# A fused attention and GEGLU kernel: block 4 in six Strassen pairs, with the loads and the attention of batches 5 to 7 moved

## The chip, the cores and the metric

The kernel runs on one core of one Trainium2 chip. The time is the device time of one execution in microseconds, and a kernel's time is the median of several executions. Times before: 305.1, 305.68 and 306.09 us, median 305.68 us.

## What is computed

First a linear attention over 8 batches, 8 heads, 576 tokens and 64 columns a head, then a gated feed-forward layer on all 4608 tokens (512 columns in, 1536 hidden, 512 out). Cut to what matters:

```python
theta = np.pi / 2 * np.arange(S) / S
phi = lambda x: concat([relu(x) * cos(theta), relu(x) * sin(theta)])   # 64 -> 128 features
kv  = einsum('bhsf,bhsd->bhfd', phi(k), v);  z = phi(k).sum(over s)
attn = (phi(q) @ kv) / (phi(q) @ z + 1e-6)
x = attn as (B * S, H * D)
out = (gelu(x @ w_gate) * (x @ w_val)) @ w_out
```

Inputs and output are float32; the matmuls take bf16.

## The kernel before

The feed-forward layer works on nine blocks of 512 tokens (n = 0 to 8). A block has 12 hidden tiles of 128 columns (jt = 0 to 11). The attention works on batches of 576 tokens, so it runs beside the feed-forward layer of earlier tokens: while block n is computed, batch n + 1 is finished and batch n + 2 is loaded and scaled. The whole order is written out by hand: the scheduler keeps each engine's instructions in the order of the code. A place in it is a slot (n, jt).

**Gate and value, two ways.** A plain unit (`gv_unit`, L425) makes one hidden tile by 8 matmuls of 512 columns (L435), one GELU (L444, ACT) and one product (L447, DVE). A pair (`Pair`, L648) makes two hidden tiles together by a Strassen scheme with 7 products of 4 matmuls of 256 columns (L659). Products 3, 5, 6 and 7 read sums of weights (S1 to S4, `w_sum`, L618), and products 4 to 7 read differences of x parts (T1 to T4, `x_sum`, L627, on POOL). Around the products ACT copies two partial sums (L678, L682) and makes two GELUs (L691, L695), and DVE makes two sums (L686, L699) and two products (L700, L704). `step` (L709) orders one pair: product 1; product 7 of the pair before it ("old", which writes its value sum to bank 6); product 5; the first slot; product 6; the old pair's product 4; product 2; numerators, where the table has one for the second slot's number; the second slot; product 3. Numerators of an even slot run only when there is no old pair. With `std` set, the step finishes its own pair, and a plain unit and a third slot follow (up to L735); the next step then has no old pair.

Blocks 3 and 4 (n < `FULL`, 5) have five pairs and two plain units (tiles 10 and 11); blocks 5 to 8 have six pairs. The sums of the weights of tiles 10 and 11 (columns from `WX` = 1280 on) lie in the stage of v, `st[:, 2]`, in its first 1024 of 2304 float32 columns (`w_part`, L603). They are made on POOL in slots (5, 7) to (5, 10), after v of batch 7, the last, has been cast out of that stage.

**A slot** (`slot`, L1133) runs `o_step` (the output layer of the block before: one Strassen product of 6 matmuls, L552, or two; h sums on POOL, L534; stores), then `attention` (L1111), then `more` (x sums and weight sums on POOL). `attention` may turn q (`TURN`: two DMA transposes on SP's queue, L224, into the one qT buffer), transpose finished rows x into the next block's xT (`turn_x`, L383, SP's queue), start loads (`LOADS`, L98, SP's queue), run the k-v unit (`KV`, L266: 72 matmuls, L272, into banks 6 and 7, two ACT copies, L281), scale q and k (`PREPS`, `LAST`: `prep_both`, L193, on ACT) and cast v (`cast_v`, L210, on POOL, into the one vx buffer).

**Numerators** (`nm_unit`, L311): for 128 tokens of a batch, 8 matmuls against qT (L313) into banks 6 and 7, then three DVE operations (L327 to L329) that write a row tile x. `NM` tells in which slot; (5, 0) there means batch 5, tokens 0 to 127.

SP's queue is one list in order: loads, stores, transposes. A DMA on it waits, among other things, for the one eight places before it to land.

Of the kernel before, what the change touches and what calls it, by code (L numbers as in the profile page):

```python
# [16 lines left out]
def kernel(  # L17
# [55 lines left out]
    def rows(t, b):  # L73
        return t[b].rearrange("(m i) (p j) d -> (i p) m (j d)", i=2, j=R)
# [5 lines left out]
    st = inp.tile([128, 3, NP, R * D], FP32)  # L80
# [25 lines left out]
    WJ, WX = 1024, 1280  # L106
# [46 lines left out]
    vx = consts.tile([128, NP, R, D + 1], BF16)  # L153
# [31 lines left out]
    def prep_both(b, part, j, eng):  # L185
        for name in "qk":
            phi_tile(name, b)
        o = phis[:, b % 2:b % 2 + 2, :, j, part * D:(part + 1) * D]
        o = o.rearrange("p a m d -> p (a m) d")
        i = st[:, 0:2, :, j * D:(j + 1) * D].rearrange("p a m d -> p (a m) d")  # L190
        tab = (cos_t, sin_t)[part]
        if eng is nc.scalar:
            nc.scalar.activation(o, i, AF.Relu, scale=tab[:, j:j + 1])  # L193
        else:
            eng.tensor_scalar(o, i, 0.0, tab[:, j:j + 1], op0=ALU.max, op1=ALU.mult)
# [13 lines left out]
    def cast_v(b, m0, m1, copy, j0=0, j1=R):  # L209
        copy(  # L210
            vx[:, m0:m1, j0:j1, 0:D],
            staged["v", b][:, m0:m1, j0 * D:j1 * D].rearrange("p m (j d) -> p m j d", d=D),
        )
# [8 lines left out]
    def turn_q(b):  # L222
        for i in range(2):
            nc.sync.dma_start_transpose(  # L224
                out=qt_tile(b)[:, i].rearrange("f m (j p) -> f (m j) p", p=64),
                in_=phi["q", b][64 * i:64 * i + 64].rearrange("p m j f -> p (m j f)"),
            )
# [38 lines left out]
    def kv_unit(b):  # L266
        kp = phi["k", b]
        for m in range(NP):
            for j in range(R):
                for i in range(2):  # L270
                    rr = slice(64 * i, 64 * i + 64)
                    nc.tensor.matmul(  # L272
                        bank(6 + i)[:, m * (D + 1):(m + 1) * (D + 1)],
                        lhsT=kp[rr, m, j, :],
                        rhs=vx[rr, m, j, :],
                        start=(j == 0),
                        stop=(j == R - 1),
                    )
# [181 lines left out]
    def flush(engs=(nc.sync, nc.sync)):  # L460
        for i, o_sb in stores:
            store(engs, i, o_sb)
        stores.clear()
# [154 lines left out]
    def w_sum(name, j0, j1, eng=nc.vector):  # L618
        x, y, op = {
            "S1": ("A21", "A22", ALU.add),  # L620
            "S2": ("S1", "A11", ALU.subtract),
            "S3": ("A11", "A21", ALU.subtract),
            "S4": ("A12", "S2", ALU.subtract),
        }[name]
        eng.tensor_tensor(w_part(name, j0, j1), w_part(x, j0, j1), w_part(y, j0, j1), op=op)
# [266 lines left out]
    def js(a, b):  # L892
# [7 lines left out]
        (2, 10): [(5, "q", 0, 5), (5, "k", 0, 5)],  # L900
        (3, 1): [(5, "q", 5, R), (5, "k", 5, R), (5, "v")],
        (3, 9): [(6, "q", 0, 5), (6, "k", 0, 5)],
        (4, 0): [(6, "q", 5, R), (6, "k", 5, R), (6, "v")],
        (4, 9): [(7, "q", 0, 5), (7, "k", 0, 5)], (4, 10): [(7, "v")],
        (5, 0): [(7, "q", 5, R), (7, "k", 5, R)],
    }
    SUMS = {
        2: {0: "1", 1: "2", 2: "34", 3: "567"},
# [6 lines left out]
    MORE = {}  # L915
# [1 line left out]
        for i in range(4):  # L917
            MORE.setdefault((n - 1, 8 + i * (n > 3)), []).append((n, i))
    for i, name in enumerate(("S1", "S2", "S4", "S3")):
        MORE.setdefault((5, 7 + i), []).insert(0, (name, WX, J))  # L920
    for i in range(4):
        MORE.setdefault((6, min(10 + i, 11)), []).append((7, i))
        MORE.setdefault((7, 8 + i), []).append((8, i))
# [12 lines left out]
    def o_step(n, jt):  # L936
# [6 lines left out]
        if jt % 3 == 1:  # L943
            flush()

    def start_loads(n, jt):
        for b, name, *part in LOADS.get((n, jt), ()):
            if len(part) == 1:
                load(nc.sync, name, b, part[0], part[0] + 2)
            elif part:  # L950
                load(nc.sync, name, b, 0, NP, *part)
            else:
                for m in (0, 2):
                    load(nc.sync, name, b, m, m + 2)
# [18 lines left out]
    def block1():  # L973
        b, n = 2, 1
        for jt in range(JT):
# [33 lines left out]
            if jt == 11:  # L1009
                nm_unit(b, 3, 6)  # L1010
            start_loads(n, jt)

    EARLY = {
# [4 lines left out]
    def early(jt):  # L1018
        for what in EARLY.get(jt, "").split():
            part = "cs".index(what[0])  # L1020
            prep_both(4, part, int(what[1]), nc.scalar if part or jt != 7 else nc.gpsimd)

    def block2():
# [54 lines left out]
        9: "s5 c5", 10: "s6", "m11": "c6", 11: "s7 c7 s8 c8",  # L1078
    }
    LAST = {  # L1080
        2: "s0 c0", 3: "s1", 4: "c1 s2", 5: "c2", 6: "s3 c3", 7: "s4", 8: "c4 s5", 9: "c5",
        10: "s6 c6", 11: "s7", 12: "c7 s8", 13: "c8",
    }
    turns = []

    def preps(n, jt):
        if n == 2:
            early(jt)
        if n in (3, 4):
            for what in PREPS.get(jt, "").split():  # L1090
                prep_both(n + 2, "cs".index(what[0]), int(what[1]), nc.scalar)
        if n in (5, 6):
            for what in LAST.get(jt + JT * (n - 5), "").split():
                prep_both(7, "cs".index(what[0]), int(what[1]), nc.scalar)

    FULL = 5
    NM = {(3, 0): (3, 4), (4, 0): (4, 4), (5, 0): (5, 4), (5, 7): (6, 0), (5, 9): (6, 1), (5, 11): (6, 2)}
    for n in (3, 4):
        NM.update({(n, 6): (n + 1, 0), (n, 8): (n + 1, 1), (n, 10): (n + 1, 2), (n, 11): (n + 1, 3)})
    LATE = {(6, 1): (6, 3), (6, 3): (6, 4)}  # L1100
    LATE.update({divmod(6 * JT + 9 + 2 * i, JT): (7, i) for i in range(NT)})

    def numerators(n, jt, at=NM):
        if (n, jt) in at:
            nm_unit(*at[n, jt])
            turns.append(at[n, jt])

    TURN = {(3, 1): 4, (4, 0): 5, (5, 0): 6, (6, 3): 7}
    KV = {(3, 1): 4, (4, 1): 5, (5, 1): 6, (6, 5): 7}

    def attention(n, jt):  # L1111
        made = list(turns)
        numerators(n, jt, LATE)
        if (n, jt) == (3, 0):
            early(JT)
        if n == 3 and 2 < jt < 7:
            w_sum(("S1", "S2", "S4", "S3")[jt - 3], WJ, WX, eng=nc.gpsimd)
        if (n, jt) in TURN:
            turn_q(TURN[n, jt])
            start_loads(n, jt)  # L1120
        for bt in made:
            turn_x(*bt)
            turns.remove(bt)
        if (n, jt) not in TURN:
            start_loads(n, jt)
        if (n, jt) in KV:
            kv_unit(KV[n, jt])
        preps(n, jt)
        m = 2 * (jt - (7 if n < 5 else 3))
        if 3 <= n <= 5 and m in (0, 2):  # L1130
            cast_v(n + 2, m, m + 2, nc.gpsimd.tensor_copy)

    def slot(n, jt):  # L1133
        o_step(*divmod(n * JT + jt - 1, JT))
        attention(n, jt)
        more(n, jt)
        if n == NB - 1 and jt in (9, 10):
            h_sum(n, jt - 9, "S3", eng=nc.gpsimd)
        if n == NB - 1 and jt == 11:
            for name in ("S1", "S2", "S4"):  # L1140
                h_sum(n, 0, name, 0, JH - 2, eng=nc.gpsimd)
# [9 lines left out]
    for n in range(3, NB):  # L1151
        jt = 0
        for T in range(JT // 2):
            std = {2: 10, 4: 11}.get(T) if n < FULL else None
            if n < FULL and T == 5:
                break
# [4 lines left out]
            jt = jts.stop  # L1161
# [17 lines left out]
    for what in (  # L1179
# [3 lines left out]
        if isinstance(what, str):  # L1183
            p = "ST".index(what[0])
# [33 lines left out]
```

## Time and profile before

| what | us |
|---|---|
| median of three runs | 305.68 |
| the profiled execution | 304.65 |
| its span, first to last instruction | 302.9 |
| PE matmuls busy | 293.1 |
| DVE busy | 229.4 |
| ACT busy | 204.8 |
| POOL busy | 174.3 |

The profile is of one execution. PE is TensorE with its matmuls, PEld its weight loads, DVE VectorE, ACT ScalarE, POOL GpSimd, SP the engine that issues most DMAs. Times within the span count from its start. A row of the timeline or of the chain of waits gives start, length, engine, line, operation, tiles written and read, and a count of merged instructions; in the chain a piece begins where the piece before it ended. The granted clock is 0.999 over the span. Block 4's first product starts at 140.7 us, block 5's at 171.4.

### The profile page before, as it was taken

How to read it: one execution, taken by the hardware profiler on the slowest of the kernel's cores; microseconds unless marked ns; L12 is line 12 of the kernel's file. 1: busy time of each engine (PE TensorE's matmuls, PEld its weight loads, DVE VectorE, ACT ScalarE, POOL GpSimd, SP SyncE). 2: the span in 40 equal slices, each digit the busy share in tenths (PEclk: the TensorE clock that was granted, in tenths of full speed). 3: DMA queues.
4: the chain of work that ended last, by engine and by line, in shares of the span. 5: the costliest groups of instructions: out<-in, count | busy, mean ns of one | idle time of the engine just before them, and what ended most of it. 6: DMA issues, size and time to landing. Idle time of an engine off the chain costs nothing.

```text
span 302.9 us, 8135 instructions
## 1 busy us (share of the span) xinstructions
PE 293.1 (97%) x3129; PEld 232.2 (77%) x3145; DVE 229.4 (76%) x500; ACT 204.8 (68%) x405; POOL 174.3 (58%) x146
## 2 busy tenths in 40 slices
PE   7799999999999999999999999999999999999993
PEld 3584456745788778797878788988888988888882
DVE  5866995998985775879587967897669785666782
ACT  7865592997574897878687868886455546555630
POOL 5585450000029999957943797769516965496310
PEclk9999999999999999999999999999999999999999
DMA  7999999989899999997897899423943241303035
GB/s 260 265 172 208 345 294 385 306 193 226 177 179 257 216 307 183 228 272 224 118 257 237 253 253 220 113 52 78 145 85 73 52 76 25 70 3 69 2 85 124
DMA packets 73175, 53.68 MB, mean 177 GB/s; under 512 B 45392, under 2 KB 62544, under 8 KB 73136
## 3 DMA queue, kind: packets, MB, share of 16 engines
q1 hardware_dynamic: 63360, 41.17, 58.9%
q0 software_dynamic: 9696, 11.93, 17.2%
q8 instruction: 24, 0.39, 0.5%
q14 instruction: 15, 0.12, 0.1%
q10 hardware_dynamic: 80, 0.07, 0.1%
HBM read 37.75 MB, written 9.44 MB: 156 GB/s over the span
## 4 chain that ended last, share of the span: by engine, by line
PE 82%; issue 5%; DVE 5%; DMA 3%; ACT 2%; POOL 1%; SPq 1%; POOLq 0%; DVEq 0%; ACTq 0%
PE ps L659 36%; PE ps L552 21%; PE ps L435 14%; PE ps L468 3%; PE ps L313 3%; DMA st<-in_v_dram 3%; PE ps L272 3%; DVE hT L447 1%; POOL st L534 1%; PE ps L235 1%; PE ps L406 1%; ACT phis L179 1%; DVE phis L181 1%; ACT gel L444 1%; PE ps L391 1%
## 5 line engine op out<-in xcount | busy, mean ns | idle before, releaser
L639 POOL TENSOR_TENSOR fs<-xT 128x512 bf16<-128x512 bf16 x14 | 16.1, 1153 | 61.1 <-ACT vx L210 43.5
L534 POOL TENSOR_TENSOR sm<-hT 128x768 bf16<-128x768 bf16 x26 | 42.7, 1643 | 14.0 <-PE ps L659 7.8
L659 PE MATMUL ps<-fs,ws 128*128 128x256 bf16 x312 | 44.5, 273 | 0.0
L659 PEld LDWEIGHTS <-ws 128*128 128x128 bf16 x416 | 39.4, 98 | 5.6 <-issue 0.5
L659 PE MATMUL ps<-xT,wg_sb 128*128 128x256 bf16 x288 | 43.2, 272 | 0.0
L699 DVE TENSOR_TENSOR ps<-fs,ps 128x512 f32<-128x512 f32 x36 | 25.0, 695 | 23.3 <-PE ps L659 22.0
L435 PE MATMUL ps<-xT,wv_sb 128*128 128x512 bf16 (+1 forms) x159 | 35.9, 347 | 0.1
L435 PE MATMUL ps<-xT,wg_sb 128*128 128x512 bf16 (+1 forms) x149 | 34.9, 345 | 0.6
L552 PEld LDWEIGHTS <-sm 128*128 128x128 bf16 x336 | 32.4, 98 | 3.9
L691 ACT ACTIVATE gel<-ps 128x512 f32<-128x512 f32 x36 | 21.4, 594 | 18.4 <-PE ps L659 18.3
L682 ACT COPY fs<-ps 128x512 f32<-128x512 f32 x36 | 21.1, 587 | 18.1 <-DVE ps L699 17.2
L659 PEld LDWEIGHTS <-wg_sb 128*128 128x128 bf16 x288 | 28.1, 98 | 4.9 <-issue 0.3
L565 DVE TENSOR_TENSOR o_sb<-sm,ps 128x256 f32<-128x256 f32 x56 | 23.4, 418 | 10.3 <-ACT sm L570 9.5
L447 DVE TENSOR_TENSOR hT<-gel,ps 128x512 bf16<-128x512 f32 (+1 forms) x40 | 23.9, 604 | 9.2 <-PE ps L435 6.8
L552 PEld LDWEIGHTS <-hT 128*128 128x128 bf16 x288 | 27.9, 98 | 3.8 <-issue 0.2
L444 ACT ACTIVATE gel<-ps 128x512 f32<-128x512 f32 (+1 forms) x40 | 21.1, 535 | 11.9 <-PE ps L435 11.0
L700 DVE TENSOR_TENSOR hT<-gel,ps 128x512 bf16<-128x512 f32 x36 | 24.7, 687 | 3.5
L534 POOL TENSOR_TENSOR sm<-hT,sm 128x768 bf16<-128x768 bf16 x12 | 19.7, 1644 | 12.9 <-PE ps L552 12.9
L695 ACT ACTIVATE gel<-ps 128x512 f32<-128x512 f32 x36 | 21.5, 598 | 7.9 <-PE ps L659 6.3
L686 DVE TENSOR_TENSOR ps<-fs,ps 128x512 f32<-128x512 f32 x36 | 24.9, 691 | 1.5 <-PE ps L659 0.8
L329 DVE TENSOR_TENSOR x_sb<-ps,rec 128x512 bf16<-128x512 f32 x36 | 24.9, 691 | 1.4 <-DVE rec L328 0.2
L193 ACT ACTIVATE phis<-st,sin_t 128x512 bf16<-128x512 f32 x36 | 25.6, 721 | 0.0
(137 smaller groups left out, 633.1 us busy)
## 6 DMA issues: line engine op xcount, KB each, us to landing
out_dram<-o_sb SPq DMA_DIRECT2D x69, 128.0 KB, 2.5
st<-in_v_dram SPq DMA_DIRECT2D x10, 576.0 KB, 6.3
st<-in_q_dram SPq DMA_DIRECT2D x5, 640.0 KB, 4.9
st<-in_q_dram SPq DMA_DIRECT2D x5, 512.0 KB, 5.2
st<-in_k_dram SPq DMA_DIRECT2D x4, 640.0 KB, 6.0
st<-in_k_dram SPq DMA_DIRECT2D x4, 576.0 KB, 4.7
st<-in_q_dram POOLq DMA_DIRECT2D x4, 576.0 KB, 12.1
st<-in_k_dram SPq DMA_DIRECT2D x4, 512.0 KB, 5.5
```

What stands on the lines that cost most here:

```text
L193: nc.scalar.activation(o, i, AF.Relu, scale=tab[:, j:j + 1])
L329: nc.vector.tensor_tensor(x, nm[:, :, :, 0:D], rec[:, :, :, None].to_broadcast([128, 2, 4, D]), op=ALU.mult,)
L435: nc.tensor.matmul(bank(to[g])[:, 0:w], lhsT=wt[:, ct, js], rhs=xt[:, ct, c0:c0 + w], start=(ct == 0), stop=(ct == CT - 1),)
L444: nc.scalar.activation(gel[:, 0:w], bank(to[0])[:, 0:w], AF.Gelu)
L447: nc.vector.tensor_mul(hT[n][:, jt, c0:c0 + w], gel[:, 0:w], bank(to[1])[:, 0:w])
L534: eng.tensor_tensor(a[name][:, j0:j1], a[x][:, j0:j1], a[y][:, j0:j1], op=op)
L552: nc.tensor.matmul(at, lhsT=hs.setdefault(key, h_parts(n, p))[a][:, j], rhs=ts[b][:, j], start=(j == 0 and i in ((1, 2, 4, 5), (1, 4, 5))[ ...
L565: nc.vector.tensor_tensor(o, got[key, k], x, op=op)
L659: nc.tensor.matmul(to[:, 256 * half:256 * half + 256], lhsT=w_part(a, j * 128, (j + 1) * 128)[:, ct], rhs=xb[self.n][b][:, ct], start=(hal ...
L686: nc.vector.tensor_tensor(bank(MIX), self.m5, self.sum, op=ALU.add)
L699: nc.vector.tensor_tensor(bank(val), self.m5, self.sum, op=ALU.add)
L700: nc.vector.tensor_tensor(self.h(1), both(gel1), both(bank(val)), op=ALU.mult)
```

## The change

Block 4 gets six pairs in place of five pairs and two plain units. For that the weight sums of tiles 10 and 11 are made in slots (4, 7) to (4, 10), so the stage of v must be free by then: v of batch 6 is loaded in slot (3, 10) in place of (4, 0) and cast in (4, 3) and (4, 4) in place of (4, 7) and (4, 8). The stage is not free again for a whole v: batch 7's is loaded in halves (two head pairs each) into columns 1024 to 2175, in (4, 10) and (5, 4), and cast in (5, 3) and (5, 7), in place of one load in (4, 10) with casts in (5, 3) and (5, 4).

Block 4's numerators move from even to odd slots: batch 5's from (4, 6), (4, 8), (4, 10), (4, 11) to (4, 5), (4, 7), (4, 9), (4, 11), and its last from (5, 0) to (5, 1). The turn of q of batch 6 moves from (5, 0) to (5, 1), and so do the later parts of q and k of batch 7. The scaling of batch 6 is spread from (4, 2) to (5, 0) and that of batch 7 from (5, 4) to (6, 2), before (5, 2) to (6, 1). Blocks 0 to 3 keep their products; blocks 6 to 8 keep their order apart from the scaling's end.

```diff
-        (4, 0): [(6, "q", 5, R), (6, "k", 5, R), (6, "v")],
-        (4, 9): [(7, "q", 0, 5), (7, "k", 0, 5)], (4, 10): [(7, "v")],
-        (5, 0): [(7, "q", 5, R), (7, "k", 5, R)],
+        (3, 10): [(6, "v")], (4, 0): [(6, "q", 5, R), (6, "k", 5, R)],
+        (4, 9): [(7, "q", 0, 5), (7, "k", 0, 5)], (4, 10): [(7, "half", 0)],
+        (5, 1): [(7, "q", 5, R), (7, "k", 5, R)], (5, 4): [(7, "half", 2)],
...
-        MORE.setdefault((5, 7 + i), []).insert(0, (name, WX, J))
+        MORE.setdefault((4, 7 + i), []).insert(0, (name, WX, J))
...
+    half = st[:, 2].rearrange("p m x -> p (m x)")[:, 1024:1024 + 2 * R * D]
+    half = half.rearrange("p (m x) -> p m x", m=2)
+    def cast_half(b, m):
+        nc.gpsimd.tensor_copy(
+            vx[:, m:m + 2, :, 0:D], half.rearrange("p m (j d) -> p m j d", d=D)
+        )
...
+            if name == "half":
+                nc.sync.dma_start(out=half, in_=rows(v, b)[:, part[0]:part[0] + 2])
+            elif len(part) == 1:
...
     LAST = {
-        2: "s0 c0", 3: "s1", 4: "c1 s2", 5: "c2", 6: "s3 c3", 7: "s4", 8: "c4 s5", 9: "c5",
-        10: "s6 c6", 11: "s7", 12: "c7 s8", 13: "c8",
+        6: {
+            2: "s0 c0", 3: "s1", 4: "c1 s2", 5: "c2", 6: "s3 c3", 7: "s4", 8: "c4 s5",
+            9: "c5 s6", 10: "c6 s7", 11: "c7", 12: "s8 c8",
+        },
+        7: {
+            16: "s0 c0", 17: "s1", 18: "c1 s2", 19: "c2", 20: "s3 c3", 21: "s4", 22: "c4 s5",
+            23: "c5 s6", 24: "c6 s7", 25: "c7", 26: "s8 c8",
+        },
...
-        if n in (3, 4):
+        if n == 3:
...
+        for b in LAST:
+            for what in LAST[b].get(jt + JT * (n - 4), "").split() if isinstance(jt, int) else ():
+                prep_both(b, "cs".index(what[0]), int(what[1]), nc.scalar)
...
-    FULL = 5
-    NM = {(3, 0): (3, 4), (4, 0): (4, 4), (5, 0): (5, 4), (5, 7): (6, 0), (5, 9): (6, 1), (5, 11): (6, 2)}
-    for n in (3, 4):
-        NM.update({(n, 6): (n + 1, 0), (n, 8): (n + 1, 1), (n, 10): (n + 1, 2), (n, 11): (n + 1, 3)})
+    FULL = 4
+    NM = {
+        (3, 0): (3, 4), (3, 6): (4, 0), (3, 8): (4, 1), (3, 10): (4, 2), (3, 11): (4, 3),
+        (4, 0): (4, 4), (4, 5): (5, 0), (4, 7): (5, 1), (4, 9): (5, 2), (4, 11): (5, 3),
+        (5, 1): (5, 4), (5, 7): (6, 0), (5, 9): (6, 1), (5, 11): (6, 2),
+    }
...
-    TURN = {(3, 1): 4, (4, 0): 5, (5, 0): 6, (6, 3): 7}
+    TURN = {(3, 1): 4, (4, 0): 5, (5, 1): 6, (6, 3): 7}
...
-        m = 2 * (jt - (7 if n < 5 else 3))
-        if 3 <= n <= 5 and m in (0, 2):
+        m = 2 * (jt - (7 if n < 4 else 3))
+        if 3 <= n <= 4 and m in (0, 2):
             cast_v(n + 2, m, m + 2, nc.gpsimd.tensor_copy)
+        if n == 5 and jt in (3, 7):
+            cast_half(7, (jt - 3) // 2)
```

On PE this makes 12 more weight loads and 12 more matmuls: 28 of 256 columns come, 16 of 512 go. `cast_half(7, 2)` is the second half's cast.

More of the change, by code (lines that the diff above doesn't have):

```diff
@@ L944, in o_step @@
             flush()
+    half = st[:, 2].rearrange("p m x -> p (m x)")[:, 1024:1024 + 2 * R * D]
[4 more added lines that the diff above has]
+        )
     def start_loads(n, jt):
         for b, name, *part in LOADS.get((n, jt), ()):
-            if len(part) == 1:
+            if name == "half":
+                nc.sync.dma_start(out=half, in_=rows(v, b)[:, part[0]:part[0] + 2])
+            elif len(part) == 1:
                 load(nc.sync, name, b, part[0], part[0] + 2)
@@ L1088, in preps @@
             early(jt)
-        if n in (3, 4):
+        if n == 3:
             for what in PREPS.get(jt, "").split():
                 prep_both(n + 2, "cs".index(what[0]), int(what[1]), nc.scalar)
-        if n in (5, 6):
-            for what in LAST.get(jt + JT * (n - 5), "").split():
-                prep_both(7, "cs".index(what[0]), int(what[1]), nc.scalar)
-    FULL = 5
-    NM = {(3, 0): (3, 4), (4, 0): (4, 4), (5, 0): (5, 4), (5, 7): (6, 0), (5, 9): (6, 1), (5, 11): (6, 2)}
-    for n in (3, 4):
-        NM.update({(n, 6): (n + 1, 0), (n, 8): (n + 1, 1), (n, 10): (n + 1, 2), (n, 11): (n + 1, 3)})
+        for b in LAST:
[3 more added lines that the diff above has]
+    NM = {
[3 rows of a table added]
+    }
     LATE = {(6, 1): (6, 3), (6, 3): (6, 4)}
```

## The prediction

> **What bounds the kernel now.** I read the page's busy times first, then the slices, then the chain of waits inside block 4, and last the queues that feed it.
>
> ```profile
> span 302.9 us, 8135 instructions
> ...
> PE 293.1 (97%) x3129; PEld 232.2 (77%) x3145; DVE 229.4 (76%) x500; ACT 204.8 (68%) x405; POOL 174.3 (58%) x146
> ...
> PE   7799999999999999999999999999999999999993
> ```
>
> PE is at nine tenths or more in 37 of 40 slices. A busy matmul row proves little by itself, because matmuls overlap, so I looked at the chain between 150 and 175 us (columns: start, length, what, count):
>
> ```profile
> 150.61 1.75 PE ps L659 x16
> 152.36 0.66 PE ps L552 x6
> 153.01 1.31 PE ps L659 x12
> 154.32 0.66 PE ps L552 x6
> ...
> 156.79 0.26 PE ps L313 x8
> 157.05 0.66 PE ps L552 x6
> 157.71 0.44 PE ps L659 x4
> 158.14 0.86 PE ps L435 x4
> ```
>
> Every piece is PE and each starts where the last ends; over the whole window the chain has 0.4% of issue and nothing of another engine. Nobody makes PE wait in block 4. So whatever leaves PE's list is gained in full, and any wait put in front of PE is lost in full; no idle time of PE is there to swallow it. The prices: 16 matmuls of 256 columns take 1.75 us, 109 ns each; 4 of 512 take 0.86, 216 ns each; the 8 of one numerator unit (L313) take 0.26 us.
>
> **Part 1: the sixth pair.** It removes tiles 10 and 11's two plain units, 2 x 8 matmuls of 512 columns (16 x 0.216 = 3.46 us), and adds a pair, 7 products x 4 of 256 columns (28 x 0.109 = 3.06 us). **PE: -0.40 us.** That is all that the change can bring, because block 4 has no PE gap to close. The Trainium skill ("TensorE: Matmul & The Clock Gate", Back-to-back issue gap) has a sustained spacing of about 131 ns at 512 columns. By that rule the plain units would take 2.1 us, and the pair would lose about 1 us; the trace has 216 ns, so the sum doesn't use it.
>
> The pair adds on ACT two copies and two GELUs (0.59 each) for two GELUs of 0.60: +1.2 us. On DVE it adds 3 operations of 0.69 and one of 0.68 for two of 0.68: +1.4 us. The cover is PE's own time. Block 5 before already runs six pairs with 18 preps (L193) in 178.0 to 187.2 at 8.16 of 9.20 us ACT busy and 6.76 DVE busy, with PE full. So I cost this at nothing, from 0 to +1.4 us.
>
> The four weight sums (L625, 4 x 1.15 us on POOL) move from block 5 into block 4. There they stand behind the last h sum (L534, which waits for a product and in the trace starts at 157.85, 1.64 long) and between the x sums (L639). S1 would end near 161 and is first used by the last pair's product 5 near 167. The last two sums share POOL with x sums that started at 166.87: four x sums and two w sums take 7 us, to about 174 if nothing is earlier, while S3 (third from the end) is wanted near 172. The numerators come a slot earlier, so the x sums do too. Cost 0; if that cover is gone, up to 1 us.
>
> **Part 2: numerators of batch 5 one slot earlier, v of batch 6 before them.** The unit (5,0) moves from slot (4,6) to (4,5). On PE that is from 156.63 to where slot 5's product starts now:
>
> ```profile
> 154.16 0.82 PE L552 MATMUL ps<-T,hT 128*128 128x256 bf16 x6
> ```
>
> It reads qT of batch 5, which SP turns by two DMA transposes (SP's timeline, then the line's own view with shortest, median and longest of each):
>
> ```profile
> 144.28 8.63 SPq L224 DMA_TRANSPOSE qT<-phis  x2
> ```
>
> ```profile
> L224 SPq DMA_TRANSPOSE qT<-phis x2: 3300/4292/5285, 144.3 to 147.6; - x2
> ...
> DMA to landing us min/median/max: 7.0/7.1/7.2
> ```
>
> The second is issued at 147.6 and lands 7.0 later, at 154.6. Before, that left 156.63 - 154.6 = 2.0 us of slack. Now PE arrives at 154.16, **0.45 us too early**, even if nothing delays the transposes. But something does. The two loads of v (576 KB each, 1.18 MB) move from behind the transposes to 138.95 (after the transpose of 1.20 us at 137.75), ahead of them in SP's queue. At the 383 GB/s that the DMAs move at 156 to 160, that is 3.1 us. What they can fill stands here (PE, PEld, DVE, ACT, POOL, clock, DMA share, GB/s):
>
> ```profile
> 141.00:142.00 1.00, 1.00 (x18) 0.92 (x16) 1.00 (x3) 0.87 (x3) 0.51 (x1) 1.00 0.01 2
> 142.00:144.00 2.00, 2.00 (x21) 1.71 (x19) 1.93 (x6) 1.31 (x3) 1.52 (x1) 1.00 0.61 138
> 144.00:146.00 2.00, 2.00 (x80) 1.73 (x78) 1.22 (x3) 0.26 (x1) 1.92 (x3) 1.00 0.58 109
> 146.00:149.00 3.00, 3.00 (x37) 2.65 (x30) 1.20 (x2) 2.20 (x6) 3.00 (x3) 1.00 1.01 154
> ```
>
> The DMAs idle 1.0 + 0.8 + 0.8 = 2.6 us from 141 to 146, and are full from 146 on with the transposes. So the v data runs from 141.0 to 144.1; two stores (256 KB, 0.7 us) and one x transpose (128 KB at 154 GB/s, 0.85 us) follow to 145.6, where the qT packets begin now at about 145.4. I take a delay of 0.3 us. Its ends: +2.1 if only the empty microsecond is filled; -1.4 if the transposes flow as those of batch 6 do (issued 174.5, the second landing 7.6 after 179.4, through a queue backed up with loads). With 0.1 us for one weight load (98 ns) before the first matmul, PE waits 0.45 + 0.3 + 0.1 = **0.85 us, from 0 to 2.7.**
>
> The Trainium skill ("DMA: Bandwidth & Descriptors", Where 436 GB/s comes from) lets transposes between SBUF and SBUF run up to 435 GB/s. By that qT's 1.18 MB would need 2.7 us and land before 150, and there would be no wait; the rows have 154 GB/s at a full DMA share, and the measurement decides.
>
> **Part 3: (5,4) from slot (5,0) to (5,1).** Block 5's first step now has an old pair to finish, so the unit follows product 2, and the kv unit of batch 6 stands in the same slot. Both write banks 6 and 7: kv must wait until DVE has read the numerators. The model is block 6's first step, which already finishes an old pair (its product 1 starts at 200.67):
>
> ```profile
> 203.61 0.69 DVE L686 TENSOR_TENSOR ps<-fs,ps 128x512 f32<-128x512 f32 x1
> 204.21 0.68 DVE L704 TENSOR_TENSOR hT<-gel,ps 128x512 bf16<-128x512 f32 x1
> ...
> 206.20 0.16 DVE L327 TENSOR_SCALAR den<-ps 128x8 f32<-128x8 f32 x1
> 206.40 0.20 DVE L328 RECIPROCAL rec<-den 128x8 f32<-128x8 f32 x1
> 206.63 0.69 DVE L329 TENSOR_TENSOR x_sb<-ps,rec 128x512 bf16<-128x512 f32 x1
> ```
>
> L704 starts 3.54 us into the step, the next operation 0.60 later, and L329 ends 1.12 after L327 starts: 5.26. PE reaches kv at six products of 0.437, one h product of 0.66, the unit of 0.26 and two h products of 1.31: 4.85. **+0.4 us**, between 0 (DVE may start L704 earlier by the 0.6 of its queue) and 0.6.
>
> **Part 4: what I cost at nothing.** qT of batch 6 is issued about 1.5 us later than 174.5, and landed at 187.0; its first reader stood at 189.4 and comes about 1 us later, so 1.5 to 2 us of slack stay. On SP the loads of q and k of batch 7, then x(5,4) and stores stand behind it; their readers come a block or several slots later. The v halves: the second waits for POOL's cast of the first (in the trace casts of that slot start at 179.65), and stands in SP's queue behind transposes that last until 184 anyway. kv of batch 7 is at 214. Preps keep their number (18 per batch) and end one slot later, one slot before the turn of batch 7. If one of these covers fails, some 0.5 to 1 us are lost.
>
> **Sum.** -0.40 + 0.85 + 0.4 = **+0.85 us.** The profiled execution takes 304.65 (its span of 302.9 and 1.75 around it); it would become 305.5. The median of the runs is 305.68, 1.03 above the profiled one, so the forecast there is **306.5 us**.
>
> **Rivals.**
>
> 1. In time after all: the transposes flow as batch 6's do, or DVE keeps up at kv. For it: -1.4 us in the bound above. Against: 0.45 us are missing before any delay. Net -0.4 to +0.3, 305.3 to 306.0. Chance 0.20.
> 2. v of batch 6 pushes the transposes: the stores and x transpose at 142 to 146 can't share with the loads, so most of 3.1 us shows up at unit (5,0). For it: the landings come in the order of issue. It decides from a delay of 0.4 us on, where the whole change loses over 0.92. Net +1.0 to +2.7, 306.7 to 308.4; middle 307.3. Chance 0.24.
> 3. ACT and DVE become the bound in block 4's last third, where they are busy 5.17 and 5.11 of 5.32 us between 166.08 and 171.40. For it: these rows. Against: six preps stand there now and four from now on. +1.2 to +1.4 on the -0.40, beside the other waits: 307.0. Chance 0.08.
> 4. The pair saves more than its matmuls, by something that these views don't show. Against: PE has no gap there. 304.5. Chance 0.06.
>
> **How the numbers follow.** The forecast's case (net +0.4 to +1.3) has 0.42. A measurement of this kernel can tell about 0.3%, 0.92 us. Slower by more: half of the forecast's case (0.20), rival 2 (0.24), most of rival 3 (0.06), 0.50. Within: 0.22 + 0.18 + 0.02 = 0.42. Faster: rival 4 and a corner of rival 1, 0.08. The range goes from -0.4 us (no wait at all) to rival 2's upper end short of its last corner: 305.2 to 308.2.
>
> **What would show it.** PE: a gap of about 0.85 us before the first L313 of block 4's third step, ended by the DMA of qT, landing near 155; a gap near 0.4 us before the kv matmuls (L272) of batch 6, ended by DVE; none elsewhere between 88 and 270 us; 12 matmuls more, and 16 fewer of 512 columns. Rival 2 shows as a landing of qT near 156 or later, rival 3 as a gap before a product 2 or 3 ended by ACT or DVE. No gap at either place makes the prediction wrong.

## The result and the profile after

Nine executions of the changed kernel have a median of **308.01 us** (307.06 to 309.91), nine of the kernel before, taken beside them, 305.59 us. The ratio is 1.008, 95% interval 1.0052 to 1.0107: slower by about 2.4 us. The profiled execution took 307.06 us against 304.65. The direction was as forecast and the time lies in the range, but the loss is nearly three times the 0.85 us of the sum.

The page of the changed kernel (span; busy time and instructions of each engine; PE by slices):

```profile
span 305.2 us, 8168 instructions
...
PE 294.2 (96%) x3143; PEld 233.7 (77%) x3157; DVE 230.8 (76%) x502; ACT 205.2 (67%) x407; POOL 174.0 (57%) x146
...
PE   7899999999999999999989999999999999999993
```

Read this page as little help: every engine has about the busy time it had, and apart from one digit at the start PE's slices differ only by the 8 in slice 21 (153 to 160 us). The waits tell more. This view lists what PE waited for from 140 us to 290 us (what waits, for what, total, times, longest); for the kernel before, the view of the same window has no line at all:

```profile
PE ps L313 <- DMA qT<-phis: 1.1, 1, 1.1
PE ps L659 <- POOL fs L639: 0.6, 1, 0.6
PE ps L659 <- ACT gel L695: 0.5, 2, 0.3
PE ps L272 <- DVE x_sb L329: 0.2, 1, 0.2
```

The first and the last are the two that the prediction named. The two in the middle are new to it. The view counts only time in which PE had nothing at all left; below I measure each wait from the starts of PE's matmuls, as the space between two starts less the usual one, which is a little more.

**The wait for qT (1.20 us).** The chain between 151 and 159 us, and the line of the transposes (shortest, median and longest time that SP was busy with one, in ns; below it the times from issue to landing):

```profile
148.82 6.35 DMA qT<-phis
...
155.21 0.40 PE ps L313 x7
```

```profile
L224 SPq DMA_TRANSPOSE qT<-phis x2: 4113/4680/5246, 143.5 to 148.8; - x2
...
DMA to landing us min/median/max: 6.3/7.2/8.0
```

The second transpose is issued at 148.8 and lands at 155.17; PE had got there at 153.96: one of the eight matmuls starts then, the other seven wait. The loads of v filled the place that the prediction read in the rows: the DMAs, idle or half idle from 141 to 146 before, now carry 363 and 359 GB/s:

```profile
141.00:142.00 1.00, 1.00 (x17) 0.91 (x14) 1.00 (x3) 0.87 (x2) 0.06 (x1) 1.00 1.11 363
142.00:144.00 2.00, 2.00 (x21) 1.71 (x19) 1.93 (x6) 1.23 (x3) 1.78 (x2) 1.00 1.02 359
```

What came late was the issue: SP was busy with the first transpose for 5.25 us (3.30 before), so the second left 1.2 us later on the span's clock. Once issued it landed in 6.35 us, no slower than before (7.0).

**Two waits for ACT (0.42 and 0.43 us).** In the chain, near the end of block 4, PE's product 5 of the last pair starts only when the GELU of L695 (of the pair before) is done, and that stood behind two scalings (L193):

```profile
165.87 1.21 ACT phis L193 x2
...
167.10 0.60 ACT gel L695
...
167.74 0.60 PE ps L659 x4
```

ACT's own timeline for the same place shows its queue. One scaling is one L193; where they follow each other, their starts are 0.62 us apart. Two more stand just ahead of L691 (from 164.16 on), and from there to L695 nothing has idle time before it, so ACT reaches L695 some 0.6 us later for each scaling put ahead of it:

```profile
165.40 0.58 ACT L691 ACTIVATE gel<-ps 128x512 f32<-128x512 f32 x1
165.87 0.72 ACT L193 ACTIVATE phis<-st,cos_t 128x512 bf16<-128x512 f32 x1
166.48 0.72 ACT L193 ACTIVATE phis<-st,sin_t 128x512 bf16<-128x512 f32 x1
167.10 0.59 ACT L695 ACTIVATE gel<-ps 128x512 f32<-128x512 f32 x1
```

The same picture stands at 202.63 to 203.17, where PE waits 0.43 us at the end of block 5. In the new table both places are the slots with "c4 s5" and "c5 s6": four scalings in one step.

**The wait at the kv unit (0.24 us).** The chain at block 5's first step ends, as predicted, L704, then the three operations of the numerators, then kv (L272):

```profile
174.98 0.59 DVE hT L704
...
175.92 0.70 DVE x_sb L329
...
176.66 1.33 PE ps L272 x72
```

**A wait in block 7 (0.80 us), which the change doesn't touch.** The first product 5 of block 7 waits for an x sum on POOL, and that for the x transpose of batch 7's first numerators:

```profile
228.68 4.10 DMA xT<-x_sb
...
232.85 1.16 POOL fs L639
...
234.05 0.60 PE ps L659 x4
```

Before, the same x sum started at 229.42, in time (POOL's timeline; the bracket is its idle time):

```profile
229.42 1.15 POOL L639 TENSOR_TENSOR fs<-xT 128x512 bf16<-128x512 bf16 x1 [9.02 <-DMA xT<-x_sb]
```

Measured from the first weight load of the numerators (7,0), the transpose is issued at +1.72 in both kernels; it lands at +4.04 before and +5.83 after. The DMAs weren't full: at 232 to 233 they moved 2 GB/s.

**The account.** To leave out the first blocks, whose waits shift block 4 by up to 4.7 us between the profiled kernels (kv of batch 5 starts at 144.4 in b2_v_early and at 149.1 in b4_pad36), I measure PE from the first kv matmul of batch 5 to the start of its last matmul, and call this the stretch. Before it takes 152.72 us, after 155.33: +2.61. The parts: -0.40 (pair) + 1.20 (qT) + 0.42 + 0.43 (ACT) + 0.24 (kv) + 0.80 (block 7) = +2.69.

That the two agree so well is in part chance, for the kernel before has a small stop of its own that the view of PE's waits doesn't list. In block 8 two groups of four weight loads are each torn apart (the brackets are idle time; the starts of PE's matmuls lose 0.30 us by it against the changed kernel, where the same groups, in the second fence, stand together):

```profile
272.29 0.10 PEld L659 LDWEIGHTS <-ws 128*128 128x128 bf16 x1
272.60 0.31 PEld L659 LDWEIGHTS <-ws 128*128 128x128 bf16 x3 [0.21 <-issue]
272.92 0.10 PEld L659 LDWEIGHTS <-wg_sb 128*128 128x128 bf16 x1
273.19 0.31 PEld L659 LDWEIGHTS <-wg_sb 128*128 128x128 bf16 x3 [0.17 <-issue]
```

```profile
274.86 0.42 PEld L659 LDWEIGHTS <-ws 128*128 128x128 bf16 x4
275.29 0.48 PEld L659 LDWEIGHTS <-wg_sb 128*128 128x128 bf16 x4
```

Of the kernels below, b1, b3 and b4 have this pause at the same place in PE's list; b2 and all that start from the changed kernel don't. What makes it was not tried. That it is missing after the change takes 0.30 us off the sum of the parts (+2.39 against the +2.61 measured), so the pair seems to bring less than 0.40; c6_final says how much.

### The profile page after: what moved, and what is told of

Same layout as the page of the kernel before. It is cut to its first block, busy times and chain, and to the rows that moved or that the text cites. A ratio compares the mean times of both kernels' runs of the same rounds, so it can differ in the third digit from the quotient of the medians.

```text
span 305.2 us, 8168 instructions
## 1 busy us (share of the span) xinstructions
PE 294.2 (96%) x3143; PEld 233.7 (77%) x3157; DVE 230.8 (76%) x502; ACT 205.2 (67%) x407; POOL 174.0 (57%) x146
## 4 chain that ended last, share of the span: by engine, by line
PE 74%; DVE 8%; DMA 6%; issue 5%; ACT 3%; POOL 1%; SPq 1%; POOLq 0%; DVEq 0%; ACTq 0%
PE ps L659 32%; PE ps L552 18%; PE ps L435 14%; PE ps L468 3%; DMA st<-in_v_dram 3%; PE ps L272 3%; PE ps L313 2%; DMA qT<-phis 2%; DVE phis L181 2%; DVE hT L447 1%; DMA xT<-x_sb 1%; ACT phis L193 1%; POOL st L534 1%; DVE ps L699 1%; PE ps L235 1%
## 5 line engine op out<-in xcount | busy, mean ns | idle before, releaser
L639 POOL TENSOR_TENSOR fs<-xT 128x512 bf16<-128x512 bf16 x14 | 16.2, 1155 | 58.8 <-ACT vx L210 43.6
L659 PE MATMUL ps<-xT,wg_sb 128*128 128x256 bf16 x296 | 44.4, 273 | 0.0
L699 DVE TENSOR_TENSOR ps<-fs,ps 128x512 f32<-128x512 f32 x37 | 25.7, 696 | 24.4 <-PE ps L659 23.0
L691 ACT ACTIVATE gel<-ps 128x512 f32<-128x512 f32 x37 | 21.9, 592 | 18.9 <-PE ps L659 18.9
L435 PE MATMUL ps<-xT,wv_sb 128*128 128x512 bf16 (+1 forms) x151 | 33.8, 345 | 0.1
L435 PE MATMUL ps<-xT,wg_sb 128*128 128x512 bf16 (+1 forms) x143 | 32.9, 343 | 0.5
L659 PEld LDWEIGHTS <-wg_sb 128*128 128x128 bf16 x296 | 28.9, 98 | 4.5 <-issue 0.3
L447 DVE TENSOR_TENSOR hT<-gel,ps 128x512 bf16<-128x512 f32 (+1 forms) x38 | 22.6, 600 | 9.3 <-PE ps L435 7.0
L700 DVE TENSOR_TENSOR hT<-gel,ps 128x512 bf16<-128x512 f32 x37 | 25.4, 688 | 3.7
L695 ACT ACTIVATE gel<-ps 128x512 f32<-128x512 f32 x37 | 22.1, 598 | 9.0 <-PE ps L659 7.3
L444 ACT ACTIVATE gel<-ps 128x512 f32<-128x512 f32 (+1 forms) x38 | 19.9, 531 | 11.8 <-PE ps L435 11.0
L686 DVE TENSOR_TENSOR ps<-fs,ps 128x512 f32<-128x512 f32 x37 | 25.6, 691 | 1.9 <-PE ps L659 1.0
L659 PE MATMUL ps<-fs,wv_sb 128*128 128x256 bf16 x172 | 25.8, 273 | 0.0
```

The source lines that it names most:

```text
L435: nc.tensor.matmul(bank(to[g])[:, 0:w], lhsT=wt[:, ct, js], rhs=xt[:, ct, c0:c0 + w], start=(ct == 0), stop=(ct == CT - 1),)
L447: nc.vector.tensor_mul(hT[n][:, jt, c0:c0 + w], gel[:, 0:w], bank(to[1])[:, 0:w])
L659: nc.tensor.matmul(to[:, 256 * half:256 * half + 256], lhsT=w_part(a, j * 128, (j + 1) * 128)[:, ct], rhs=xb[self.n][b][:, ct], start=(hal ...
L686: nc.vector.tensor_tensor(bank(MIX), self.m5, self.sum, op=ALU.add)
L691: nc.scalar.activation(self.gel0, self.other, AF.Gelu)
L695: nc.scalar.activation(gel1, bank(MIX), AF.Gelu)
```

## The experiments

**The theory.** Four separate causes, of which each has its own repair. (A) qT lands too late for the earlier numerators, partly since v of batch 6 goes ahead of it. (B) Four scalings in one step hold ACT's GELU back; it is their order, not ACT's load. (C) Numerators and kv in one step. (D) PE's 24 added instructions (12 weight loads, 12 matmuls) move the points at which PE's next instructions are fetched, and one fetch then falls on the x transpose. The page lists a DMA queue "q8 instruction" of 24 fetches with 16 KB each; one comes 3.81 us after the start of numerators (7,0) in the changed kernel, before the transpose lands, and 4.74 after it in the kernel before, when the transpose (at 4.04) has landed. **The rivals:** ACT is simply fuller by the pair's 1.2 us (against B); the block 7 wait comes from the moved loads, transposes or POOL work (against D); v doesn't matter to qT (against half of A).

**e1_preps: the changed kernel with the scalings spread**, so that no step has four; the last three of each batch stand in one slot, (5,0) and (6,2).

```diff
-            9: "c5 s6", 10: "c6 s7", 11: "c7", 12: "s8 c8",
+            9: "c5", 10: "s6 c6", 11: "s7", 12: "c7 s8 c8",
...
-            23: "c5 s6", 24: "c6 s7", 25: "c7", 26: "s8 c8",
+            23: "c5", 24: "s6 c6", 25: "s7", 26: "c7 s8 c8",
```

> The change with one scaling step (of slots 9 and 21+2 of the batches 6 and 7: s6, and what follows it) moved one slot later, so that slots 8 and 9 hold three scalings in place of four. Theory (four scalings in two neighbouring slots make the last GELU of the pair late, and PE waits for it before product 5 of the next pair): the two waits of 0.42 us at 167.2 and 202.6 us both go, 0.84 us less than the changed kernel, near 307.2. Rival (ACT is full in that third of the block anyhow, by the pair's added copies and GELUs): the waits move a slot or two on and the time stays near 308.0.

307.1 us, ratio to before 1.0055 (1.0034 to 1.0077); stretch 154.00. Both waits of 0.42 are gone. ACT's timeline at the place of the first:

```profile
165.17 0.58 ACT L691 ACTIVATE gel<-ps 128x512 f32<-128x512 f32 x1
165.64 0.72 ACT L193 ACTIVATE phis<-st,cos_t 128x512 bf16<-128x512 f32 x1
166.41 0.60 ACT L695 ACTIVATE gel<-ps 128x512 f32<-128x512 f32 x1
```

One L193 between L691 and L695, not two. The work is the same, so ACT's load isn't the cause. A new wait of 0.32 us stands at 212.2, in the step that now has "c7 s8 c8": there L695 stands behind three L193, L691 and a copy of the output layer (L570), which ACT does without a pause from 209.37 on.

**e2_product_first: the changed kernel with the output product ahead of numerators (5,0).**

```diff
-        (4, 0): (4, 4), (4, 5): (5, 0), (4, 7): (5, 1), (4, 9): (5, 2), (4, 11): (5, 3),
+        (4, 0): (4, 4), (4, 7): (5, 1), (4, 9): (5, 2), (4, 11): (5, 3),
...
-    LATE = {(6, 1): (6, 3), (6, 3): (6, 4)}
+    LATE = {(4, 5): (5, 0), (6, 1): (6, 3), (6, 3): (6, 4)}
```

> The change with the numerators (5, 0) behind the output product of slot (4, 5) in place of before it: 0.66 us later on PE. Theory (PE waits there for qT to land, and for nothing else): the wait of 1.20 us shrinks by 0.66 to about 0.55 us, 307.35. Rival (the DMA transposes are not what it waits for, or they land later when less waits for them): the wait stays near 1.2 us and the time near 308.0.

307.27 us, 1.0063 (1.004 to 1.0085); stretch 154.19. The qT wait falls to 0.36 us, the other four waits stay (0.43, 0.24, 0.43, 0.48). In PE's waits from 140 to 290 us, qT's line goes from 1.1 to

```profile
PE ps L313 <- DMA qT<-phis: 0.2, 1, 0.2
```

So the wait is 0.84 us shorter: 0.66 of it because PE gets there that much later, the rest because qT lands a little earlier in this profile (10.51 us after the kv unit's start, 10.70 in the changed kernel). It is the time of arrival that counts.

**e3_v_behind: the changed kernel with v of batch 6 loaded behind the transposes again**, cast in slot (4,7).

```diff
-        (3, 10): [(6, "v")], (4, 0): [(6, "q", 5, R), (6, "k", 5, R)],
+        (4, 0): [(6, "q", 5, R), (6, "k", 5, R), (6, "v")],
...
-        if 3 <= n <= 4 and m in (0, 2):
+        if n == 3 and m in (0, 2):
...
+        if (n, jt) == (4, 7):
+            for m in (0, 2):
+                cast_v(6, m, m + 2, nc.gpsimd.tensor_copy)
```

> The change with v of batch 6 loaded in slot (4, 0) again, behind the turn of q of batch 5, and cast in slot (4, 7), both halves; the weight sums follow. Theory (most of the 1.2 us wait is the slot that the numerators moved forward, 0.45 to 0.55 us, and the rest, 0.6 us, is v in front of the transposes): the second transpose lands near 154.3 on the span's clock in place of 155.2 and the wait is 0.5 to 0.6 us; the time falls by 0.6 us to 307.4 if POOL, with 2.3 us of casts now between the h sums and the weight sums, still has S3 in time. Rival (the load in front costs nothing, since the DMAs were idle there): the wait stays near 1.2 us, 308.0. Second rival (v in front is all of it): the wait goes, 306.8.

307.71 us, 1.0075 (1.0047 to 1.0103); stretch 154.92. The qT wait is 0.57 us and the landing 10.07 us after the kv unit's start (10.70 in the changed kernel). Nobody waits for the later cast. Block 7's wait is 1.0 us here, so v wasn't its cause. This single landing says little, because it scatters. Over all profiled kernels the second transpose lands at 9.30, 9.45, 9.50, 9.81, 10.07 and 10.22 with v behind it (mean 9.73) and at 9.97, 10.00, 10.08, 10.16, 10.22, 10.51, 10.70 and 11.14 with v ahead (mean 10.35): **v ahead costs 0.6 us of landing, with a scatter of about 0.5 either way** (the 95% interval of the difference, over 6 and 8 kernels with one profile each, is 0.2 to 1.1). The issue of the second transpose moves by more, from 2.8 to 4.0 us in the mean. PE arrives at about 9.5 in the changed kernel (10.70 less its wait of 1.20; e3 gives the same, 10.07 less 0.57).

**e4_kv_later: the changed kernel with kv of batch 6 a step later.**

```diff
-    KV = {(3, 1): 4, (4, 1): 5, (5, 1): 6, (6, 5): 7}
+    KV = {(3, 1): 4, (4, 1): 5, (5, 3): 6, (6, 5): 7}
```

> The change with the k-v unit of batch 6 in slot (5, 3) in place of (5, 1), two slots behind the numerators (5, 4) with which it shares banks 6 and 7. Theory: the gap before its first matmul goes from 338 ns to the 96 ns that every k-v unit has, 0.24 us less, 307.8; no new wait, as the numerators that need it stand in (5, 7). Rival (it pays at the new place, since the old pair's value sum holds bank 6 there): 308.0 or more.

308.12 us, 1.0071 (1.0045 to 1.0097): as a time inconclusive, the interval holds the changed kernel's own ratio. In the trace the wait is gone: from 160 to 200 us PE's waits are

```profile
PE ps L659 <- ACT gel L695: 0.3, 1, 0.3
```

alone, and there is no new one at kv's new place. The qT wait is 0.66 us, block 7's 0.57, the stretch 154.40.

**b1_bunched: the kernel before, with only the new order of batch 7's scalings**, so without a pair in block 4.

```diff
-  8: "c4 s5", 9: "c5", 10: "s6 c6", 11: "s7", 12: "c7 s8", 13: "c8"
+  8: "c4 s5", 9: "c5 s6", 10: "c6 s7", 11: "c7", 12: "s8 c8"
```

> The kernel before, with only the changed kernel's order of the scalings for batch 7 from the ninth slot on (four scalings in two neighbouring slots). Theory: one wait of 0.42 us for the last GELU of a pair appears in block 5, 306.0. Rival (the changed kernel's waits come from its sixth pair, not from the order of the scalings): no wait and no change, 305.6.

306.09 us beside 305.21 (ratio 1.0019, 0.9999 to 1.0038); stretch 152.96. One wait appears, 0.42 us long, in the step of the four scalings, with the same chain:

```profile
196.82 1.21 ACT phis L193 x2
...
198.04 0.60 ACT gel L695
...
198.69 0.60 PE ps L659 x4
```

With e1 this settles B from both sides: the order alone makes the wait without the pair, and the order alone takes it away with the pair.

**b3_pad12: the kernel before, with 12 one-column matmuls at the very start** (12 weight loads and 12 matmuls, as many PE instructions as the change adds; nothing reads what they make).

```diff
+  for _ in range(12):
+      nc.tensor.matmul(bank(5)[0:1, 0:1], lhsT=dummy[:, 0:1], rhs=dummy[:, 0:1], start=True, stop=True)
```

> The kernel before, with 12 matmuls of one column (24 instructions of PE, as many as the change adds) at the very start, where PE waits for the first v. Theory (the wait before product 5 of block 7 comes from the instruction fetch of PE, one 16 KB DMA each 256 instructions, which 24 more instructions move to 3.5 us after the numerators (7, 0), in front of the x transpose that block 7's x sums wait for; before it comes at 4.7 us, when that has landed): the fetch moves to 3.3 to 3.9 us, the transpose lands 5.4 to 6.0 us after those numerators in place of 4.0, and PE waits 0.4 to 1.0 us there: 306.2. Rival (the transposes are late because of the moved loads, casts or turns): the landing stays at 4.0 us and the time at 305.6.

306.78 us, ratio 1.004 (1.0022 to 1.0059): slower than before by 1.2 us, by instructions that compute nothing used, 224 us ahead of the place that pays (8.9 against 232.9 us). The fetch comes 3.64 us after numerators (7,0), the x transpose lands at 5.90 in place of 4.04, and PE waits 0.87 us. Stretch 153.72:

```profile
228.40 4.17 DMA xT<-x_sb
...
232.64 1.16 POOL fs L639
...
233.84 0.60 PE ps L659 x4
```

**e5_pad36: the changed kernel with 36 such matmuls**, which should carry the fetch to the other side.

> The changed kernel, with 36 matmuls of one column at the very start, which move PE's instruction fetches 72 instructions forward. Theory (same as for the 12 before): the fetch comes about 0 us after the numerators (7, 0), before the transpose is issued at 1.7 us, so the transpose lands at 4.0 to 4.5 us and the wait before product 5 of block 7 (0.8 us in the changed kernel's profile, 0.36 to 1.0 in the four experiments) goes: 0.4 to 0.8 us less, 307.4, if no fetch lands on another transpose. Rival (order of the moved work): the wait stays, 308.0.

306.73 us, 1.0064 (1.0038 to 1.009); stretch 153.95. The fetch now comes 0.83 us ahead of numerators (7,0), the transpose lands at 4.04 as in the kernel before, and the line "POOL fs L639" is gone from PE's waits from 140 to 290 us:

```profile
PE ps L659 <- ACT gel L695: 0.5, 2, 0.3
PE ps L313 <- DMA qT<-phis: 0.3, 1, 0.3
PE ps L272 <- DVE x_sb L329: 0.2, 1, 0.2
```

A small one of 0.27 us came at 236.65, behind DVE (L704). Adding instructions to the kernel before makes the wait, adding more to the changed kernel removes it: D holds, and the rival, that the moved DMAs or POOL work did it, falls. All profiled kernels fall in two groups (times in us after the first weight load of numerators (7,0); the transpose is issued at 1.72, in c6_final at 1.86):

| fetch begins | kernels: fetch, landing |
|---|---|
| between issue and landing | e1 3.30, 5.39; c1 3.35, 5.41; e2 3.34, 5.51; e4 3.30, 5.60; after 3.81, 5.83; b3 3.64, 5.90; e3 3.63, 6.04 |
| earlier or later | e5 -0.83, 4.04; c5 -0.65, 4.03; b4 0.48, 4.03; c6 4.22, 4.16; b1 4.60, 4.03; b2 4.67, 4.03; before 4.74, 4.04 |

Another x transpose, issued between 206 and 212 us, shows the same in the same fourteen profiles. In the eleven where a fetch begins 1.1 to 2.4 us after its issue, it takes 3.6 to 4.3 us to land; in the three with 36 added matmuls (e5, b4, c5) no fetch begins under way, and it takes 2.41 us.

The ratio of e5, 1.0064 against the changed kernel's 1.008, points the same way without deciding it; the qT wait is 0.47 here.

**b4_pad36: the kernel before with the 36 matmuls**, to see what these cost by themselves.

> Control: the kernel before with the 36 one-column matmuls at the start. Theory: the fetch moves to about 1 us after the numerators (7, 0), before the transpose is issued, so there is no wait in block 7, and the matmuls stand where PE waits for the first v: 305.4 to 305.9. Rival (the added matmuls cost their own time, some 2 us): 307.5.

306.26 us beside 305.41, 1.002 (0.9994 to 1.0046); stretch 152.72, exactly that of the kernel before, and no wait in block 7. But the profiled execution has a wait of 2.06 us at 93.6 us for qT of batch 3, outside the stretch. It isn't shown to come from the padding: e3, which has none, has one of 1.6 us in the same place, at 94.4. The padding is used here as a probe, not as a repair.

**c1_preps_nm_kv: e1, e2 and e4 together.**

> Three of the repairs together: scalings spread, numerators (5, 0) behind the output product, k-v unit of batch 6 in slot (5, 3). Theory (the waits add up): -0.84 - 0.65 - 0.24 from the changed kernel; -0.40 for the pair, +0.35 for qT and +0.55 for the x transpose of block 7 are left, 0.5 us above the kernel before, 306.1. Rival (a wait that goes is followed by another): 307 or more.

306.25 us beside 305.21, 1.0033 (1.0006 to 1.0061); stretch 153.00. The waits for qT, at kv and for the four scalings are gone, and 0.33 us at 213.0 (three scalings in slot (6,2)) and 0.39 us in block 7 are left. The repairs add up.

**c5_pad36: e2 and e4, another spread of the scalings (batch 7's begin a slot earlier, at (5,3)), and the 36 matmuls.**

> All repairs together: scalings spread (batch 7's one to two a slot from (5, 3) on, so that block 6 has no wait for a GELU either, which the first spreading got there: 0.33 us), numerators (5, 0) behind the output product, k-v unit of batch 6 in slot (5, 3), 36 one-column matmuls at the start against the instruction fetch. Theory (four waits and the pair make up all of the change): only the pair's -0.40 is left, and PE's time from the k-v unit of batch 5 to its last matmul is 152.3 us, against 152.7 before and 155.3 in the changed kernel; 305.0 against 305.4 before. Rival (the sixth pair costs something by itself): 153 us or more there, 306.

305.87 us beside 305.41, 1.0015 (0.9991 to 1.0038); stretch 153.49, against the 152.3 that the theory expected. Two waits spoil it. qT landed at 11.14, the latest of all, and cost 0.99 us in spite of the output product. And the first scaling moved into slot (5,3), where the kv unit's copies (L281) already stand in ACT's queue, made a new wait of 0.59 us:

```profile
183.39 0.38 ACT kv_sb L281
183.77 0.33 ACT phis L193
...
184.28 0.60 ACT gel L695
...
184.93 0.60 PE ps L659 x4
```

So my repair had the same fault as the change: it was made by counting scalings, without looking at what else ACT has in that step.

**b2_v_early: the kernel before with only v of batch 6 loaded in slot (3,10).**

> The kernel before, with the load of v of batch 6 in slot (3, 10), in front of the turn of q of batch 5, and nothing else. Theory (v in front delays the transposes by 0.3 to 0.6 us): the second transpose lands 10.2 to 10.4 us after the k-v unit of batch 5 begins, in place of 9.8, and as its reader comes 2 us later than in the changed kernel, the time stays: 305.4. Rival (v in front is worth all of the 1.2 us): 11.0 us.

304.87 us beside 305.41, 0.9971 (0.9947 to 0.9994); stretch 152.42. qT lands at 10.00, a little earlier than expected, and nobody waits, since the numerators stand where they stood. The early load by itself isn't a cost; it becomes one when PE comes for qT at 9.5. The stretch is 0.30 us shorter than before because the pause in block 8 is missing; the rest of the gain in time lies outside the stretch and has no explanation here.

**c6_final: the changed kernel with all causes taken away and no padding**: e2, e3 and e4, the scalings spread, with one unit of batch 7's (k, 8) given to POOL, and numerators (7,0) ahead of their output product, so that the x transpose is out earlier.

```diff
-            23: "c5 s6", 24: "c6 s7", 25: "c7", 26: "s8 c8",
+            23: "c5", 24: "s6 c6", 25: "s7", 26: "c7 s8",
...
+        if (n, jt) == (5, 11):
+            prep_both(7, 0, 8, nc.gpsimd)
...
-    LATE.update({divmod(6 * JT + 9 + 2 * i, JT): (7, i) for i in range(NT)})
+    LATE.update({divmod(6 * JT + 9 + 2 * i, JT): (7, i) for i in range(1, NT)})
+    NM[6, 9] = (7, 0)
```

> The sixth pair of block 4 with every wait taken out by place and not by padding: v of batch 6 behind the transposes again (cast in slot (4, 7)), numerators (5, 0) behind the output product, scalings spread (and one of batch 7's on POOL, in (5, 11)), k-v unit of batch 6 in (5, 3), numerators (7, 0) ahead of the output product of slot (6, 9), 0.66 us earlier. Theory (four waits and the pair are all of the change): PE's time from the k-v unit of batch 5 to its last matmul is 152.3 to 152.6 us, against 152.7 before; time 305.0 to 305.4 against 305.4 before, which a measurement can hardly tell from no change. Rival (each place that is freed brings another wait, as in the kernel with all repairs and the padding): 153.2 us or more, 306.

305.14 us beside 305.23, 0.9996 (0.9981 to 1.0012). From 140 to 290 us PE waits for nothing; these are all its waits, and each of them is in the first blocks:

```profile
PE ps L159 <- POOL ws L134: 1.5, 1, 1.5
PE ps L752 <- DMA st<-in_v_dram: 0.8, 1, 0.8
PE ps L406 <- DMA wv_sb<-in_moe_w_val_dram: 0.6, 1, 0.6
PE ps L391 <- DVE x_sb L329: 0.2, 1, 0.2
PE ps L249 <- DVE vx L210: 0.2, 1, 0.2
```

The stretch is 152.15 us, 0.57 shorter than before and 3.18 shorter than in the changed kernel. Of the 0.57, 0.30 is the pause in block 8, which this kernel doesn't have; against b2_v_early, which doesn't have it either, c6_final is 0.27 shorter. So the pair brings some 0.3 us once nothing waits; but that is 0.1% of the kernel, and no time measured here can tell it from nothing. Block 7 is clear by little: the fetch begins 0.06 us after the x transpose has landed.

## Why the prediction was right or wrong

**What bounds the kernel: right.** "Any wait put in front of PE is lost in full": the five waits add up to 3.09 us. With the pair at -0.27 and the missing pause at -0.30 that makes +2.52, within 0.1 us of the stretch's +2.61.

**Part 1, the pair's -0.40 us: right in its cause, a third too large.** c6_final against b2_v_early has 0.27, one profile each; where the other 0.13 goes was not found. The price of 216 ns for a matmul of 512 columns, kept against the Trainium skill's 131 ns ("TensorE: Matmul & The Clock Gate", Back-to-back issue gap), held: by an estimate from the page's figure the pair would have cost about 1 us, and c6_final, without other waits, should have been longer in the stretch. **ACT and DVE at nothing: failed for ACT,** and this is the larger miss (0.85 us in two places). The step was "Block 5 before already runs six pairs with 18 preps ... with PE full. So I cost this at nothing", and in Part 4 "Preps keep their number (18 per batch) and end one slot later". I compared sums of ACT's busy time with the time at hand. What counts is the queue of one step: in block 4's steps three scalings make no wait and four make one. Rival 3 named the right place (a product waiting for ACT, block 4's end) but gave the wrong reason, a full ACT, and set it aside with another sum, "six preps stand there now and four from now on"; b1_bunched shows the wait without the pair. DVE and the **weight sums on POOL** stayed hidden, as costed.

**Part 2, qT: the right wait, with two terms off.** Forecast 0.85 us, 1.20 in the profiled execution, 0.47 to 0.72 in three other kernels with the same two causes (e5, e4, e1). The terms: PE came 9.50 us after the kv unit's start, and landings with v behind scatter from 9.30 to 10.22 about 9.73, so the slot costs 0.2 us on average, and 0.45 was the case of the one landing that I read (9.81, and PE at 9.36). The delay by v was put at 0.3; the means give 0.6, which by the prediction's own bound (0.4) is rival 2's case, though that rival's sign, a landing near 156, didn't come (155.17). In the profile the delay shows as a later issue of the second transpose, not as a slower one. That 0.2 and 0.6 come near the forecast 0.85 again is luck. What the range for this term lacked was not an end but the scatter: the wait is not a fixed number. The Trainium skill's 435 GB/s for these transposes ("DMA: Bandwidth & Descriptors", Where 436 GB/s comes from), by which nothing would wait, isn't borne out: the second transpose landed 6.35 us after its issue, and the wait is there.

**Part 3, kv: right,** 0.24 against 0.4, and 0.36 in e1_preps.

**Part 4, the covers: right one by one, but for the preps.** qT of batch 6 was issued 1.06 us later in the stretch (30.78 against 29.72) and yet landed 1.25 earlier (before it landed at 187.17, not at 187.0 as I read; nothing rests on that). POOL waits 2.2 us for the second half of v, but PE waits neither for that nor for the later q and k. **"None elsewhere between 88 and 270 us": wrong.** Beside ACT's two waits stands block 7's 0.80 us. The sum had no term for the number of instructions itself, though the page lists the fetches as a DMA queue. In the six profiled kernels that have the changed instruction count and numerators (7,0) in their old place block 7's wait is 0.36 to 1.0 us, so it belonged in the range; the place of the fetch next to each tightly timed transpose would have shown it.

In short: forecast +0.85, plus ACT 0.85, plus block 7 0.80, plus 0.35 for qT, less 0.16 at kv, is +2.69, of which the stretch shows +2.61. That 308.01 still lies in the range is luck: its upper end stood for rival 2 (net up to +2.7 us, most of it at qT) and was filled by two causes that the sum had at nothing or not at all.

## What to carry to other kernels

On an engine that issues in order, a sum of busy time over a stage doesn't show whether a wait appears: when work is regrouped, write out the queue of that engine for the fullest step and look for the instruction that the bounding engine waits for. Instructions added to the bounding engine also move its instruction fetches behind them: in b3_pad12 a transfer that had landed just in time became late 224 us further on, and unused instructions at the start (a pad) are a cheap probe for it. A sum of waits that fits should be checked against a second kernel without them, as a small pause in the kernel before can make it fit by chance. A gain of 0.1% from less work is worth trying only where each of the added waits can be taken out too; here repairs in five places were needed to come back to the same time.

## What the runs showed of the hardware

PE's instructions are fetched by DMAs of 16 KB on a queue of their own, 24 in the whole execution, so one for some 260 of the 6300 instructions that the page counts for PE and PEld; that they are PE's is seen from b3, b4 and e5, where added PE instructions move them. When a fetch begins while an x transpose of 128 KB is under way, that transpose lands 5.4 to 6.0 us after the numerators' start in place of 4.04, at its end with the DMAs nearly idle (share 0.02 at 232 to 233 us in the changed kernel). That the fetch's place decides was shown by moving it in both directions; through what it holds the transpose up (one of the 16 DMA engines, or an order among queues) was not tried.

The landing of one and the same pair of qT transposes scatters between kernels whose code up to there is the same or nearly so: from 9.30 to 10.22 us with v behind it, from 9.97 to 11.14 with v ahead. A wait that depends on it is not one number: 0.47 to 1.20 us in the kernels that have the changed order and no output product in front.
